# Moving VectorE's waiting instructions later in program order: evacuation, maximum, pick and transposed P between the block transposes of a decode-attention kernel

## The chip, the cores and the metric

The kernel runs on one core of one Trainium2 chip. Times are device microseconds (us) of that core, quoted as medians of the runs; a profiled execution gives the trace ("the span" is the time from its first to its last instruction, 1.2 to 2.5 us less than the run's time in these runs). The experiments ran in several rounds on different chips; the kernel before was timed again in each round, with medians of 438.63 to 439.46 us.

## The reference

Two independent problems A and B of the same shape are computed and their outputs concatenated. Each is one decode step of attention over a sliding window of the last 4096 positions of a cache, batch 2, 32 query heads, 16 key heads of width 128:

```python
q = (x @ wq).reshape(B, Sq, Hq, Dh).transpose(0, 2, 1, 3)       # B=2, Sq=1, Hq=32, Dh=128
k = repeat(k_cache[:, :, Sk - W:, :], rep, axis=1)              # W=4096, rep=2, bf16
v = repeat(v_cache[:, :, Sk - W:, :], rep, axis=1)
p = softmax(einsum("bhqd,bhkd->bhqk", q, k) * Dh ** -0.5)
o = einsum("bhqk,bhkd->bhqd", p, v).transpose(0, 2, 1, 3).reshape(B, Sq, Hq * Dh) @ wo
```

The work per byte is small. What matters is that 153.1 MB (the caches' windows, wq and wo) have to be read once from HBM, the memory that holds the inputs. The loads bring them into SBUF, and the matmuls put their results into PSUM; these are the core's two memories in which the kernel declares its buffers (`sbuf_tensor`, `psum_tensor`).

## The kernel before

The caches are cut into 16 slabs (4 key heads of one batch element, 4.19 MB of K and as much of V each). Two slabs, one per batch element, make a group G; there are 8 groups, and one load of wo (1.18 MB) for each. Step `t` handles K slab `t` and V slab `i = t - 3`. An even step is the first of a pair, an odd one the second.

In a step, VectorE transposes the two halves of the K slab in blocks (X0, X1), and TensorE multiplies each half into the scores (S0, S1, 16 matmuls of 512 columns each). Then follow, for a group: the maximum (VectorE), two tiny GpSimd steps and a transpose on TensorE (Tm), its reduction (nM), a broadcast back through TensorE and the bias for the exponential (VectorE), the exponential on ScalarE (about 5 us), the block transpose of P (pT, VectorE), the sums (a matmul and VectorE), PV on TensorE, its evacuation from PSUM (VectorE, two instructions), a matmul that gathers the diagonal blocks (dg), its pick (VectorE: A, then oP), and the output projection (TensorE).

VectorE needs half of `xt` free before it can transpose into it, so X(t, h) waits for S(t-1, h). The program order of each engine is the order of the calls in this loop:

```python
for t in range(NSLAB + LAG):                # NSLAB = 16, LAG = 3
    i = t - LAG; odd = t % 2 == 1; live = t < NSLAB
    Gb = t // 2 - 1 if not odd and t >= 2 and t <= NSLAB else None
    Gd = (t - 5) // 2 if odd and t >= 5 else None
    if live:
        make_X(t, 0); make_S(t, 0)
    if Gb is not None: make_bias(Gb)        # TensorE, then VectorE; the exponential behind it
    if Gd is not None: make_dg(Gd)          # TensorE, then VectorE (pick: A, oP)
    if live:
        make_X(t, 1); make_S(t, 1); ...
    if live and odd: make_max(t // 2)
    if Gb is not None: make_rsum(Gb); make_pT(Gb); make_sums(Gb)
    ...
    if i >= 0: make_PV(i); make_evac(i)
    if Gd is not None and Gd != NG - 2: make_proj(Gd) ...
    if live and odd: make_Tm(t // 2)        # with nM
```

The loads of K, V and wo are issued by SyncE, in one fixed order; a load whose buffer is still in use waits for a semaphore before it is issued (in the profile before SyncE stood 254.0 us in 16 waits for a transpose to free a slab's buffer, and 43.9 us in 5 waits in front of loads of wo). A ring of four buffers takes K and V slabs. wo has two buffers, so the load of wo G waits for projection G - 2:

```python
stream = []
for t in range(NSLAB + LAG):
    if t < NSLAB: stream.append(("K", t))
    if t >= LAG:
        i = t - LAG
        if i % 2 == 0 and i // 2 < NG - 2: stream.append(("W", i // 2))
        stream.append(("V", i))
...
def issue(key):
    if kind == "W":
        deps = [proj_op[i - 2]] if i >= 2 else []
    ...
    deps = [last_reader[prior[-1]]] if prior else first_deps[r]
```

## Time and profile before

| | before |
|---|---|
| time | 439.75 us (3 runs, 437.0 to 440.02), span of the profiled run 437.3 us |
| HBM read | 153.10 MB, 350 GB/s over the span |
| TensorE / VectorE busy | 57% / 49% of the span |
| a pair of steps, 153.0 to 204.3 us | 51.3 us |
| mean granted TensorE clock (1 is full speed) | 0.801 |

No engine is busy for much more than half the time. The chain that ended last, part 4 of the page, says that it passes through TensorE and VectorE in turn and hardly through DMA:

```profile
PE 52%; DVE 36%; DMA 8%; POOL 1%; ACT 1%; issue 1%; SPq 0%; DVEq 0%
```

The waits of VectorE in the kernel before (who waited for whom: total us, times, longest us) show where it stands:

```profile
DVE mx L456 <- PE st L242: 44.3, 8, 6.5
DVE tmp L551 <- PE tb L548: 43.6, 8, 7.1
DVE bias L474 <- PE tb L471: 39.7, 8, 6.0
DVE ssum L504 <- PE tb L501: 24.5, 7, 3.8
```

L456 is the maximum, L551 the first half of the pick (A), L474 the bias, L504 the sums. The timeline of VectorE in one pair (start us, duration us, line, what is written and read, idle time before it and its releaser) shows what these waits hold up:

```profile
152.98 4.42 DVE L422 STREAM_TRANSPOSE xt<-ring 128x4096 f32<-128x4096 f32 x1
162.93 0.23 DVE L474 SCALAR_TENSOR_TENSOR bias<-vmask,tb,offm 128x4 f32<-128x4 f32 x1 [5.53 <-PE tb L471]
163.08 4.44 DVE L422 STREAM_TRANSPOSE xt<-ring 128x4096 f32<-128x4096 f32 x1
...
177.76 4.43 DVE L422 STREAM_TRANSPOSE xt<-ring 128x4096 f32<-128x4096 f32 x1
189.14 0.42 DVE L551 TENSOR_TENSOR tmp<-tb,cm 128x256 f32<-128x256 f32 x1 [6.94 <-PE tb L548]
189.60 0.61 DVE L558 TENSOR_REDUCE oP<-tmp 128x16 bf16<-128x256 f32 x1
190.12 4.44 DVE L422 STREAM_TRANSPOSE xt<-ring 128x4096 f32<-128x4096 f32 x1
200.12 1.22 DVE L456 TENSOR_REDUCE mx<-st 128x2 f32<-128x1024 f32 x1 [5.56 <-PE st L242]
```

Read the first three lines: X0 ends at 157.4, and X1 could follow at once, its data lie in SBUF. But bias stands in front of it in program order, its input comes from a tiny transpose on TensorE (0.22 us, at 162.68) behind all of S0, and so X1 starts at 163.08. In the odd step the pick does the same. TensorE in turn stands still while X1 runs (its next group, at 167.57, had waited 4.68 us for it). The two engines take turns.

DMA follows from that: a buffer comes free late, so a load starts late. SyncE issues the loads (SPq is its queue), and the longest entry in its list of waits is the wait for a transpose to free a buffer:

```profile
SPq L369 <- DVE xt L422: 254.0, 16, 20.3
```

The windows view of a pair (window, its length, busy us and count of TensorE, its weight loads, VectorE, ScalarE and GpSimd, then granted clock, DMA share, GB/s):

```profile
205.00:256.00 51.00, 29.19 (x150) 7.04 (x110) 26.16 (x17) 4.98 (x8) 1.94 (x8) 0.80 0.84 352
```

From 5 to 135 us the same view gives 429 GB/s.

### The profile page before, as it was taken

Reading aid. Unit: us, or ns where it says so; the run is one execution under the profiler, and the core shown is the slowest. Engines: PE = TensorE matmul, PEld = TensorE weight load, DVE = VectorE, ACT = ScalarE, POOL = GpSimd, SP = SyncE. Lnnn points to the kernel's source line nnn. Section 1 sums busy time; section 2 is a strip of 40 time slices with the busy share of each in tenths; the row PEclk is TensorE's granted clock in tenths of the full one; section 3 lists DMA queues with packets and bytes.
Section 4 is the critical chain, followed back from the end, with each engine's and each line's share of the span. In section 5 each row is a group of like instructions: output and inputs, shape, how many; then the busy total and the mean of one; then the engine's idle time right before and its main releaser. Section 6 shows DMA issues by size and latency. Waiting matters only on the chain.

```text
span 437.3 us, 2617 instructions
## 1 busy us (share of the span) xinstructions
PE 247.6 (57%) x1299; PEld 60.3 (14%) x937; DVE 214.6 (49%) x138; ACT 44.4 (10%) x77; POOL 21.6 (5%) x82
## 2 busy tenths in 40 slices
PE   0553835494535845446466555368554474656487
PEld 0110101120111211011011111112111110111122
DVE  0207854645654345546443466534465455544343
ACT  1020004000400003000300004000040003100400
POOL 3000010000000000001000010000000010000100
PEclk9995988876876788769886688967888698866759
DMA  8999999999995898949989498967989497895900
GB/s 348 442 419 432 430 421 446 432 432 442 399 408 255 336 423 354 408 174 396 429 360 405 153 441 355 414 288 291 440 363 405 171 406 339 336 432 215 376 9 2
DMA packets 6660, 153.28 MB, mean 351 GB/s; under 512 B 748, under 2 KB 888, under 8 KB 1272
## 3 DMA queue, kind: packets, MB, share of 16 engines
q1 hardware_dynamic: 6628, 153.10, 83.3%
q8 instruction: 9, 0.15, 0.1%
q14 instruction: 3, 0.02, 0.0%
q10 hardware_dynamic: 20, 0.01, 0.0%
HBM read 153.10 MB, written 0.00 MB: 350 GB/s over the span
## 4 chain that ended last, share of the span: by engine, by line
PE 52%; DVE 36%; DMA 8%; POOL 1%; ACT 1%; issue 1%; SPq 0%; DVEq 0%
DVE xt L422 30%; PE st L448 20%; PE st L242 18%; DMA ring<-in_A_k_cache_dram 8%; PE ot L520 8%; DVE oR L542 2%; PE pj L583 2%; PE pj L242 2%; DVE tmp L541 1%; ACT pR L481 1%; PE tb L548 1%; DVE oP L558 1%; POOL zq L414 1%; PE tb L501 1%; DVE tmp L551 1%
## 5 line engine op out<-in xcount | busy, mean ns | idle before, releaser
L448 PE MATMUL st<-xt,zq 128*128 128x512 bf16 x256 | 132.3, 517 | 151.7 <-DVE xt L422 151.7
L422 DVE STREAM_TRANSPOSE xt<-ring 128x4096 f32<-128x4096 f32 x32 | 141.5, 4431 | 20.4 <-DMA ring<-in_A_k_cache_dram 18.5
L242 PE MATMUL st<-xt,zq 128*128 128x512 bf16 x256 | 129.1, 504 | 0.0
L481 ACT ACTIVATE pR<-st,bias 128x512 bf16<-128x512 f32 x32 | 39.7, 1402 | 305.6 <-DVE bias L474 305.6
L448 PEld LDWEIGHTS st<-xt,zq 128*128 128x128 bf16 x256 | 31.0, 121 | 280.1 <-DVE xt L422 160.7
L520 PE MATMUL ot<-ring,pT 128*32 128x512 bf16 x512 | 33.9, 412 | 0.0
L456 DVE TENSOR_REDUCE mx<-st 128x2 f32<-128x1024 f32 x8 | 9.8, 1225 | 44.3 <-PE st L242 44.3
L551 DVE TENSOR_TENSOR tmp<-tb,cm 128x256 f32<-128x256 f32 x8 | 3.4, 425 | 43.6 <-PE tb L548 43.6
L414 POOL TENSOR_TENSOR zq<-qs,bmask 128x64 bf16<-128x64 bf16 x32 | 8.7, 293 | 304.1 <-PE st L242 288.3
L490 DVE STREAM_TRANSPOSE pT<-pR 128x2048 bf16<-128x2048 bf16 x8 | 18.5, 2311 | 9.8 <-ACT pR L481 9.8
L541 DVE SCALAR_TENSOR_TENSOR tmp<-ot,rsb,dmask 128x512 f32<-128x512 f32 x16 | 12.0, 751 | 19.5 <-PE ot L520 19.5
L474 DVE SCALAR_TENSOR_TENSOR bias<-vmask,tb,offm 128x4 f32<-128x4 f32 x8 | 1.8, 227 | 39.7 <-PE tb L471 39.7
L542 DVE TENSOR_REDUCE oR<-tmp 128x128 f32<-128x512 f32 x16 | 16.4, 1026 | 0.6
L583 PE MATMUL pj<-wob,oP 128*2 128x288 bf16 x63 | 15.8, 286 | 0.5 <-DVE oP L558 0.5
L242 PE MATMUL pj<-wob,oP 128*2 128x288 bf16 x63 | 15.8, 286 | 0.0
L520 PEld LDWEIGHTS ot<-ring,pT 128*32 128x32 bf16 x512 | 12.8, 102 | 19.7 <-issue 10.4
L504 DVE TENSOR_REDUCE ssum<-tb 128x2 f32<-128x8 f32 x8 | 1.3, 162 | 24.5 <-PE tb L501 24.5
L275 PE MATMUL ot<-ring,pT 128*32 128x512 bf16 x36 | 8.3, 448 | 3.3 <-DMA ring<-in_B_wq_dram 2.8
L252 PE MATMUL tb<-ident_b,pR 8*128 8x8 bf16 x9 | 0.7, 199 | 15.3 <-DVE pR L213 15.3
L501 PE MATMUL tb<-rsum,m 128*128 128x8 f32 x16 | 3.2, 273 | 10.6 <-POOL rsum L495 10.6
L481 ACT ACTIVATION_READ_ACCUMULATOR pR<-st,bias 128x1 f32 x32 | 8.7, 271 | 0.0
L242 PE MATMUL pj<-ring,pT 128*32 128x512 bf16 x36 | 8.2, 444 | 0.0
(57 smaller groups left out, 62.1 us busy)
## 6 DMA issues: line engine op xcount, KB each, us to landing
ring<-in_A_k_cache_dram SPq DMA_DIRECT2D x8, 4096.0 KB, 24.1
ring<-in_A_v_cache_dram SPq DMA_DIRECT2D x8, 4096.0 KB, 16.6
ring<-in_B_k_cache_dram SPq DMA_DIRECT2D x8, 4096.0 KB, 12.8
ring<-in_B_v_cache_dram SPq DMA_DIRECT2D x7, 4096.0 KB, 14.8
ring<-in_A_wq_dram SPq DMA_DIRECT2D x1, 4608.0 KB, 13.6
ring<-in_B_wq_dram SPq DMA_DIRECT2D x1, 4608.0 KB, 24.0
wob<-in_A_wo_dram SPq DMA_DIRECT2D x4, 1152.0 KB, 12.3
wob<-in_B_wo_dram SPq DMA_DIRECT2D x3, 1152.0 KB, 6.3
```

The costliest lines, as they stand in the source:

```text
L242: return e.add_instruction(mybir.InstMatmult(name=nc.get_next_instruction_name(), engine=mybir.EngineType.PE, ins=[e.lower_ap(mv_), e.lowe ...
L275: last = e.matmul(o, wt, mv_, start=first, stop=True, skip_group_check=True)
L414: last = e.tensor_tensor(dst, src, msk, ALU.mult)
L422: Xop[(t, jh)] = dve(lambda e: e.transpose(xt[:, jh, :].bitcast(FP32).rearrange("p (kp x kt) -> p x kp kt", kp=2, kt=2), ring[:, r, jh * H ...
L448: last = e.matmul(ob, wt, mv_, start=first, stop=True, skip_group_check=True)
L456: ch[(G, "max")] = dve(lambda e: e.tensor_reduce(mx[:], st[:, :].rearrange("p (x t) -> p t x", t=2), AX.X, ALU.max), [Sop[(2 * G + 1, 1)]] ...
L481: last = e.activation(pR[:].rearrange("p (x k) -> p k x", k=4)[:, kv, :], st[:, :].rearrange("p (x t) -> p t x", t=2)[:, kv % 2, :], ACTF.Exp,
L490: pT_op[G] = dve(lambda e: e.transpose(pT[:, v, :].rearrange("p (w j q) -> p j w q", w=4, q=8), pR[:].rearrange("p (j w q) -> p j w q", w= ...
L520: last = e.matmul(OTB[32 * c:32 * c + 32, :], pT[:, v, base + 32 * c:base + 32 * c + 32], ring[:, r, jj * 128:(jj + 4) * 128], start=rd == ...
L541: evac_op[i] = dve(lambda e: e.scalar_tensor_tensor(tv, o, rsb[:, v, b:b + 1], dm, ALU.mult, ALU.mult), deps, "ev%d" % i)
L542: ch[(G, "red%d" % b)] = dve(lambda e: e.tensor_reduce(oR[:, b, :], tmp[:].rearrange("p (j d) -> p d j", j=4), AX.X, ALU.add), [evac_op[i] ...
L583: e.matmul(PJ[0], wt, wob[:, v, j, 0:NH], start=start and j == 0, stop=True, skip_group_check=True)
```

## The change

The intent is to put on VectorE, between X0 and X1, only work whose input is already there when X0 ends, and to move the instructions that wait for TensorE behind X1. For that, four things move down: the evacuation of PV(i) from the end of its step to the next step's gap, the maximum from the end of its odd step and the pick from the gap of its odd step to the gap of the next even step, and pT from its even step to the gap of the next odd step. The projection, which needs the pick, moves along; the dg matmul moves from the gap to the end of its odd step, Tm and nM follow the maximum, and the sums follow pT. Bias and sums stand behind X1. The diff, cut to its core (the maker functions are only split so that their TensorE and VectorE halves can be called apart):

```diff
             if live:
                 make_X(t, 0)
                 make_S(t, 0)
-            if Gb is not None:
-                make_bias(Gb)
-            if Gd is not None:
-                make_dg(Gd)
+            if 0 <= i - 1 and t <= NSLAB:
+                make_evac(i - 1)
+            if Gp is not None and not last:       # Gp = (t - 6) // 2, even steps
+                make_pick(Gp)
+            if Gc is not None:                    # Gc = (t - 2) // 2, even steps
+                make_max(Gc)
+            if Gs is not None:                    # Gs = (t - 3) // 2, odd steps
+                make_rsum(Gs)
+                make_pT(Gs)
+            if Gc is not None:
+                make_Tm_pe(Gc)
             if live:
                 make_X(t, 1)
                 make_S(t, 1)
 ...
-            if live and odd:
-                make_max(t // 2)
-            if Gb is not None:
-                make_rsum(Gb)
-                make_pT(Gb)
-                make_sums(Gb)
+            if Gc is not None:
+                make_nM(Gc)
+            if Gs is not None:
+                make_sums(Gs)
+            if Gd is not None:                    # Gd = (t - 5) // 2, odd steps
+                make_dg(Gd)
 ...
+            if Gp is not None and not last:
+                make_proj(Gp)
+ ...
+            if Gc is not None:
+                make_bias(Gc)
 ...
             if i >= 0:
                 make_PV(i)
-                make_evac(i)
-            if Gd is not None and Gd != NG - 2:
-                make_proj(Gd)
- ...
-            if live and odd:
-                make_Tm(t // 2)
+                if t >= NSLAB:
+                    make_evac(i)
```

More of the change, by code (lines that the diff above doesn't have):

```diff
@@ L397, in build_kernel @@
         ch = {}
+        tm_job = {}
+        dg_job = {}
         prev = lambda G, k: [ch[(G - 1, k)]] if (G - 1, k) in ch else []
@@ L459, in make_max, with make_Tm_pe, make_nM @@
             ch[(G, "pick")] = pool(lambda e: e.tensor_tensor(m1[:], mv[:, 0:1], mv[:, 1:2], ALU.add), [ch[(G, "mult")]] + prev(G, "Tm"), "pick%d" % G)
-        def make_Tm(G):
+        def make_Tm_pe(G):
             n, b, op = tb_job(lambda e, bank: e.transpose(bank[0:1, 0:128], m1[:, 0:1], ident_f[:]), "Tm%d" % G, [ch[(G, "pick")], p_ident_f])
             ch[(G, "Tm")] = op
+            tm_job[G] = (n, b)
+        def make_nM(G):
+            n, b = tm_job[G]
+            op = ch[(G, "Tm")]
             nm = dve(lambda e: e.tensor_reduce(nM[0:1, 0:16], b[0:1, 0:128].rearrange("o (a w) -> o w a", a=8), AX.X, ALU.max, negate=True),
@@ L550, in make_dg, with make_pick @@
             ch[(G, "dg")] = op
+            dg_job[G] = (n, bank)
+        def make_pick(G):
+            v = G % 2
+            n, bank = dg_job[G]
+            op = ch[(G, "dg")]
             a = dve(lambda e: e.tensor_tensor(
@@ L605, in build_kernel @@
             live = t < NSLAB
-            Gb = t // 2 - 1 if not odd and t >= 2 and t <= NSLAB else None
+            Gc = (t - 2) // 2 if not odd and t >= 2 else None
+            Gs = (t - 3) // 2 if odd and t >= 3 else None
             Gd = (t - 5) // 2 if odd and t >= 5 else None
+            Gp = (t - 6) // 2 if not odd and t >= 6 else None
+            if Gc is not None and Gc >= NG:
+                Gc = None
+            if Gs is not None and Gs >= NG:
+                Gs = None
+            last = t == NSLAB + LAG - 1
             if live:
@@ L619, in build_kernel @@
                     make_Z(t + 2)
-            if live and odd:
-                make_max(t // 2)
-            if Gb is not None:
-                make_rsum(Gb)
-                make_pT(Gb)
-                make_sums(Gb)
-            if t == NSLAB + LAG - 1:
+            if Gc is not None:
[4 more added lines that the diff above has]
+                make_dg(Gd)
+                if Gd == NG - 2:
+                    make_pick(Gd)
+            if Gp is not None and not last:
+                make_proj(Gp)
+                if (Gp + 1) % GP == 0:
+                    make_E(Gp // GP)
+            if Gc is not None:
+                make_bias(Gc)
+            if last:
                 filler(4)
@@ L629, in build_kernel @@
                 make_PV(i)
-                make_evac(i)
-            if Gd is not None and Gd != NG - 2:
-                make_proj(Gd)
-                if (Gd + 1) % GP == 0:
-                    make_E(Gd // GP)
-            if live and odd:
-                make_Tm(t // 2)
+                if t >= NSLAB:
+                    make_evac(i)
         filler(3)
@@ L639, in build_kernel @@
         make_dg(NG - 1)
+        make_pick(NG - 1)
         filler(3)
```

## The prediction

> What bounds the kernel now. The steps run in series. In the chain of waits the transposes take 30% of the span, the score matmuls 38%, and DMA only 8%. In the timeline from 153.0 to 204.3 us one pair of steps takes 51.3 us. VectorE is busy for only about 26.2 us of such a pair, TensorE for 29.2 (windows view). The list of VectorE's waits says why: in each pair it stands at bias for 5.5 us, at the pick's first half (A) for 6.9, at maximum for 5.6, at the sum for 3.6, at the evacuation for about 2.1. Each waits for a TensorE result queued behind score matmuls, and the next 4.43 us transpose stands behind it. [...]the trace agrees (after 5.5 us idle bias starts at 162.93 and the transpose behind it at 163.08).
>
> DMA: 429 GB/s from 5 to 135 us, then 352 in each pair, with holes
>
> What changes. No work is added or removed. Bias (even steps) and A (odd steps) leave the place between the two transposes; evacuation, pick, maximum and pT go there, by which time their inputs are done. Expected compute time from the first transpose's start:
> - odd step: 4.45 + evacuation 1.8 + pT 2.35 + 4.45 = 13.1, second score group about 5.1, sums and reciprocal 0.6: 18.8.
> - even step: 4.45 + 1.8 + pick 1.05 + maximum 1.25 + 4.45 = 13.1, score group 5.1, projection 2.1, bias 0.5: 20.8.
> A pair: 39.6 us instead of 51.3. The bias and the sums still stand in front of the next first transpose, so half of the serialization remains.
>
> A pair moves 17.96 MB (4 slabs of 4.19 MB and one wo of 1.18): 41.8 us at 429 GB/s. So DMA becomes the bound.
>
> A new wait: the projection also moves, from an odd step to the end of the next even step. The in-order DMA queue holds wo behind projection G-2, and behind wo stand the next V and K. So once in a pair the queue runs nearly dry: K of the even step lands, 20.2 us of step to the projection, 1.2 us from issue to the first bytes, then wo, V, K, 22.2 us: about 44 us a pair.
>
> Sum. Until K6 lands DMA is saturated: 53.7 MB, about 126 us. Four pairs of 44 (K14 at 302), then K15 and the last four V without wo in between; exp, pT, PV in series after K15, and V15 can only be issued after PV13: last PV at about 369, and from there 8.5 us to the end as before. Span 378, time 379 us.
>
> PREDICTED time 379 us, range 367 to 392. Faster by over 2% 0.97, within 2% 0.02, slower 0.01.
>
> What would show it: VectorE waits for bias and sums only at the step's end, 5 to 7 us each; transposes appear as waiting for DMA in even steps; the DMA queue's largest waits are wo for the projection in each pair; pairs of 42 to 45 us.
>
> What would make it wrong: the TensorE clock (0.5 after idle, the score group 3.8 to 6.9 us by it; [...]here 0.43 us per matmul, then 0.24); warm second groups give 42 us pairs and about 370. Cold ones give 46 and 390. A longer tail.

Two passages that did not come from a trace or run of this case are cut and marked. No term of the sum goes with them: it still comes to a span of 378 us and a time of 379. What the trace of the kernel before shows of the hardware that the prediction speaks of:

- The clock: the granted clock was 0.50 from 157.4 to 160.4 us, at 0.43 us from matmul to matmul, and 1.00 from 160.7 to 162.6, at 0.24. Each of the 22 score groups from 130.60 to 397.30 us began at 0.40 to 0.43 us from matmul to matmul, after TensorE had stood idle for 4.68 to 6.27 us. The range of 3.8 to 6.9 us for a group is an estimate: sixteen times 0.24 and sixteen times 0.43.
- From issue to the first bytes: a load of K was issued at 194.59 us, and DMA moved 0 GB/s until 195.80: 1.2 us.
- The order of the loads: wo was issued at 152.56 us, V at 152.94 and K at 167.54, in the order of the list.

## The result

| | before | after |
|---|---|---|
| time, median | 439.19 us (4 runs, 437.0 to 440.02) | 381.36 us (4 runs, 380.03 to 383.39) |
| HBM read over the span | 350 GB/s | 401 GB/s |
| a pair of steps | 51.3 us | 44.2 us (129.29 to 306.18 us are four pairs) |
| mean granted TensorE clock | 0.801 | 0.848 |

The ratio is 0.869, with a 95% interval of 0.864 to 0.875. The result is correct.

The profiled spans differ by 55.9 us. Counted by the start of the even X0 of steps 6 and 14 (152.98 and 357.94 us before, 129.29 and 306.18 after), 23.7 us of this lie before step 6, 28.1 in the four pairs from there, and 4.1 after step 14 begins.

The chain that ended last now goes mostly through DMA:

```profile
DMA 50%; DVE 22%; PE 18%; issue 7%; ACT 1%; SPq 1%; POOL 0%; DVEq 0%
```

The waits of VectorE after the change. The pick and the maximum are gone from the top; the transposes (L424) now wait for DMA:

```profile
DVE bias L481 <- PE tb L478: 43.1, 7, 7.6
DVE ssum L511 <- PE tb L508: 37.4, 7, 6.8
DVE xt L424 <- DMA ring<-in_A_k_cache_dram: 27.0, 4, 18.1
DVE xt L424 <- DMA ring<-in_B_k_cache_dram: 21.5, 6, 5.6
```

The timeline of VectorE in a pair after the change:

```profile
129.29 4.45 DVE L424 STREAM_TRANSPOSE xt<-ring 128x4096 f32<-128x4096 f32 x1 [5.00 <-DMA ring<-in_A_k_cache_dram]
...
136.46 1.22 DVE L458 TENSOR_REDUCE mx<-st 128x2 f32<-128x1024 f32 x1
137.59 4.44 DVE L424 STREAM_TRANSPOSE xt<-ring 128x4096 f32<-128x4096 f32 x1
...
149.69 0.23 DVE L481 SCALAR_TENSOR_TENSOR bias<-vmask,tb,offm 128x4 f32<-128x4 f32 x1 [7.51 <-PE tb L478]
149.84 4.44 DVE L424 STREAM_TRANSPOSE xt<-ring 128x4096 f32<-128x4096 f32 x1
...
155.91 2.30 DVE L497 STREAM_TRANSPOSE pT<-pR 128x2048 bf16<-128x2048 bf16 x1
158.13 4.40 DVE L424 STREAM_TRANSPOSE xt<-ring 128x4096 f32<-128x4096 f32 x1
168.10 0.17 DVE L511 TENSOR_REDUCE ssum<-tb 128x2 f32<-128x8 f32 x1 [5.57 <-PE tb L508]
...
174.04 4.45 DVE L424 STREAM_TRANSPOSE xt<-ring 128x4096 f32<-128x4096 f32 x1 [5.57 <-DMA ring<-in_B_k_cache_dram]
```

Between X0 and X1 VectorE never waits. One wait per step is left, at its end (bias in even steps, sums in odd ones), and the even step's X0 then waits for its K slab. The compute part of the pair is 20.55 us (129.29 to 149.84) and 18.6 us (149.84 to 168.4), 39.2 us; the rest of the 44.75 us of this pair is waiting for DMA.

That DMA is not full shows in windows of one us in the same pair (the last two columns are DMA's share and GB/s):

```profile
146.00:147.00 1.00, 1.00 (x6) 0.19 (x2) 0.00 (x0) 0.00 (x0) 0.00 (x0) 1.00 0.27 98
147.00:148.00 1.00, 1.00 (x8) 0.25 (x4) 0.00 (x0) 0.00 (x0) 0.47 (x2) 1.00 0.08 33
148.00:149.00 1.00, 1.00 (x11) 0.36 (x5) 0.00 (x0) 0.00 (x0) 0.60 (x2) 1.00 0.00 0
149.00:150.00 1.00, 1.00 (x14) 0.42 (x14) 0.31 (x2) 0.05 (x1) 0.00 (x0) 1.00 0.00 0
```

And this is what ends the hole, in SyncE's timeline. The load of wo comes first, at 149.53, when the projection on TensorE is done; a V slab and a K slab are issued right behind it, though their buffers had long been free (the V load's since PV ended at 126.7 us, the K load's since X1 ended at 142.0):

```profile
149.53 0.33 SPq L353 DMA_DIRECT2D wob<-in_A_wo_dram  x1
149.91 0.54 SPq L369 DMA_DIRECT2D ring<-in_A_v_cache_dram  x1
150.49 0.61 SPq L369 DMA_DIRECT2D ring<-in_B_k_cache_dram  x1
```

In SyncE's own list of waits this one (L353 issues wo; it is put down to the last TensorE instruction before it, the bias's transpose) is the longest:

```profile
SPq L353 <- PE tb L478: 134.3, 5, 30.2
```

### The profile page after: what moved, and what is told of

Same layout as the page of the kernel before. It is cut to its first block, busy times and chain, and to the rows that moved or that the text cites. A ratio compares the mean times of both kernels' runs of the same rounds, so it can differ in the third digit from the quotient of the medians.

```text
span 381.4 us, 2626 instructions
## 1 busy us (share of the span) xinstructions
PE 236.0 (62%) x1299; PEld 58.6 (15%) x937; DVE 212.2 (56%) x138; ACT 44.7 (12%) x77; POOL 22.0 (6%) x82
## 4 chain that ended last, share of the span: by engine, by line
DMA 50%; DVE 22%; PE 18%; issue 7%; ACT 1%; SPq 1%; POOL 0%; DVEq 0%
DMA ring<-in_A_k_cache_dram 25%; DMA ring<-in_B_k_cache_dram 25%; DVE xt L424 13%; PE st L450 5%; PE st L242 5%; PE pj L596 2%; PE pj L242 2%; DVE oR L549 2%; DVE mx L458 2%; PE ot L527 2%; DVE tmp L548 2%; ACT pR L488 1%; DVE pT L497 1%; DVE oP L571 1%; DVE tmp L564 1%
## 5 line engine op out<-in xcount | busy, mean ns | idle before, releaser
L450 PE MATMUL st<-xt,zq 128*128 128x512 bf16 x256 | 124.1, 485 | 109.1 <-DVE xt L424 109.1
L424 DVE STREAM_TRANSPOSE xt<-ring 128x4096 f32<-128x4096 f32 x32 | 141.6, 4431 | 49.8 <-DMA ring<-in_A_k_cache_dram 27.0
L242 PE MATMUL st<-xt,zq 128*128 128x512 bf16 x256 | 122.6, 479 | 0.0
L450 PEld LDWEIGHTS st<-xt,zq 128*128 128x128 bf16 x256 | 29.4, 115 | 234.1 <-DVE xt L424 125.9
L527 PE MATMUL ot<-ring,pT 128*32 128x512 bf16 x512 | 32.3, 396 | 0.0
L596 PE MATMUL pj<-wob,oP 128*2 128x288 bf16 x63 | 17.3, 305 | 0.5 <-DVE oP L571 0.5
L242 PE MATMUL pj<-wob,oP 128*2 128x288 bf16 x63 | 17.3, 306 | 0.0
L275 PE MATMUL ot<-ring,pT 128*32 128x512 bf16 x36 | 8.9, 477 | 2.2 <-DMA ring<-in_B_wq_dram 1.7
L213 DVE TENSOR_TENSOR pR<-tmp,hmask 8x1152 bf16<-8x1152 bf16 x1 | 1.3, 1347 | 12.7 <-DMA tmp<-in_B_x_dram 12.7
L555 PE MATMUL tb<-oR,selx 128*128 128x256 f32 x16 | 6.1, 466 | 3.3 <-DVE ssum L511 3.3
```

What stands on the lines that cost most here:

```text
L242: return e.add_instruction(mybir.InstMatmult(name=nc.get_next_instruction_name(), engine=mybir.EngineType.PE, ins=[e.lower_ap(mv_), e.lowe ...
L275: last = e.matmul(o, wt, mv_, start=first, stop=True, skip_group_check=True)
L424: Xop[(t, jh)] = dve(lambda e: e.transpose(xt[:, jh, :].bitcast(FP32).rearrange("p (kp x kt) -> p x kp kt", kp=2, kt=2), ring[:, r, jh * H ...
L450: last = e.matmul(ob, wt, mv_, start=first, stop=True, skip_group_check=True)
L527: last = e.matmul(OTB[32 * c:32 * c + 32, :], pT[:, v, base + 32 * c:base + 32 * c + 32], ring[:, r, jj * 128:(jj + 4) * 128], start=rd == ...
L596: e.matmul(PJ[0], wt, wob[:, v, j, 0:NH], start=start and j == 0, stop=True, skip_group_check=True)
```

## The experiments

The theory has three parts: the time came from VectorE's order (T1); the changed kernel is held by DMA and by the wo load in its queue (T2); the granted clock only sets the length of the links of the chain (T3). Rivals are named at each run. Each heading says on which kernel the edit was made.

### e1: the wo load one step later (on after)

```diff
-                if i % 2 == 0 and i // 2 < NG - 2:
+                if i % 2 == 1 and i // 2 < NG - 2:
                     stream.append(("W", i // 2))
```

> The kernel after the change, with each wo load put one step later in the DMA queue (behind K of the next even step, before the second V of its pair), nothing else. Theory (the queue is held each pair by the wo load that waits for the projection of two groups before): the five SP waits of about 30 us for the projection vanish, the hole in DMA once a pair (121 GB/s at 145 to 150 us) vanishes, a pair of steps takes 41.8 us instead of 44.2, and the time falls by five times 2.4 us to about 369 us. Rival (the hole comes from the ring of four slots or from the compute chain, wo only stands in it): SP waits the same time at the next V or K, time 379 to 383 us.

Measured: 369.97 us, ratio to before 0.844 (0.841 to 0.848). The pairs took 41.66, 41.64, 41.68 and 41.65 us (126.53 to 293.16 us), and the windows view of one of them shows DMA full:

```profile
210.00:252.00 42.00, 29.24 (x166) 7.19 (x118) 26.31 (x17) 5.01 (x8) 2.19 (x8) 0.80 1.01 433
```

SyncE's waits for the projection fell from 134.3 to 40.1 us in total, and DMA no longer runs dry:

```profile
SPq L353 <- PE tb L478: 40.1, 5, 13.3
```

So the hole came from the place of wo in SyncE's order of loads, not from the four ring buffers: the same ring now keeps DMA full. The profiled span is 13.4 us shorter (381.4 to 368.0): 2.8 us of it before the even X0 of step 6, where the second wo load no longer stands in front of K6, and 10.3 us in the four pairs. This supports T2, with the number expected (41.8 us, 369 us).

### e2: the same wo move in the kernel before

The diff is that of e1, made on the kernel before.

> The kernel before with the same one-step-later wo load. Theory: the kernel before is bound by its compute chain of 51.3 us a pair, so keeping DMA fuller is worth nothing: 436 to 441 us. Rival (DMA order was a limit in the kernel before too): 10 us or more faster.

Measured: 439.78 us, ratio 1.002 (0.999 to 1.005). The kernel before was not held by the order of its loads; the same edit that saves 11 us after the change saves nothing before it.

### e3: the pick alone (on before)

```diff
-            if Gd is not None:
-                make_dg(Gd)
             if live:
                 make_X(t, 1)
                 make_S(t, 1)
                 ...
+            if Gd is not None:
+                make_dg(Gd)
```

> The kernel before with only the dg matmul and the pick (A, oP) moved from between the two transposes of an odd step to behind the second score group. Theory (VectorE's order is what serializes): the wait of 6.9 us at A between the transposes goes, the second transpose follows the first, the two score groups of odd steps run back to back, a pair takes 44 to 45 us instead of 51.3, time about 385 to 395 us. Rival (all moves are needed together; the wait just moves to the next instruction, the maximum): within 2% of 439 us.

Measured: 394.85 us, ratio 0.900 (0.897 to 0.903), pairs of 44.4 us (215.69 to 260.07). In VectorE's timeline the two transposes of the odd step now follow each other (one merged line of 8.76 us):

```profile
215.69 8.76 DVE L422 STREAM_TRANSPOSE xt<-ring 128x4096 f32<-128x4096 f32 x2
229.59 0.42 DVE L551 TENSOR_TENSOR tmp<-tb,cm 128x256 f32<-128x256 f32 x1 [5.14 <-PE tb L548]
```

The wait did not move on in full: A waits 5.14 us behind both transposes, and the maximum behind it no longer waits. Moving the pick (two instructions a pair, with their dg matmul) gives 44 of the 58 us. One other cure was not run: dg ahead of S0 on TensorE, with the pick where it was. The rival, that only all the moves together pay, falls. In the pairs the pick alone even gives what the whole change gives, 44.4 us against 44.2, where the changed kernel is held by its wo load. The changed kernel's profiled span is 12.8 us shorter, and this comes from the time before step 6, whose even X0 starts at 129.29 us instead of 145.12, less 3.6 us lost after step 14 begins.

### e4: the bias alone (on before)

```diff
-            if Gb is not None:
-                make_bias(Gb)
 ...
             if live:
                 make_X(t, 1)
                 make_S(t, 1)
                 ...
+            if Gb is not None:
+                make_bias(Gb)
             if live and odd:
                 make_max(t // 2)
```

> The kernel before with only the bias moved from between the two transposes of an even step to behind the second score group; pT stays in the same step. Theory: the wait at bias goes, but pT then stands on VectorE waiting for the whole exponential (about 5 us) with the next transposes behind it, so the even step gets about 2 us longer (24.8 to 26.7): 445 to 460 us. Rival (every move of a waiting instruction out of the gap between transposes pays by itself): about 5 us per pair less, 395 to 405 us.

Measured: 439.84 us, ratio 1.003 (0.999 to 1.007): no gain, which excludes the rival, but not the loss that I had put a number on either. VectorE's timeline:

```profile
202.38 8.75 DVE L422 STREAM_TRANSPOSE xt<-ring 128x4096 f32<-128x4096 f32 x2
215.97 0.23 DVE L474 SCALAR_TENSOR_TENSOR bias<-vmask,tb,offm 128x4 f32<-128x4 f32 x1 [4.84 <-PE tb L471]
221.20 2.31 DVE L490 STREAM_TRANSPOSE pT<-pR 128x2048 bf16<-128x2048 bf16 x1 [5.01 <-ACT pR L481]
```

pT, still in the same step, stands waiting for the whole exponential, 5.01 us, and eats what the bias gave. The even step took 25.0 us (202.38 to 227.41) instead of 24.8; I had expected 26.7. So moving the bias alone does not pay, and the change moves pT with it; that the two moved without the other instructions would pay was not run.

### e5: the end of the kernel reordered (on e1)

```diff
+            end = t == NSLAB
+            if end: make_max(Gc)                  # before evacuation and pick
-            if 0 <= i - 1 and t <= NSLAB:
+            if 0 <= i - 1 and t < NSLAB:
                 make_evac(i - 1)
 ...
                 make_nM(Gc)
+            if end:
+                make_bias(Gc)                     # before the projection of group 5
+                make_evac(i - 1)
```

> e1_wo_later with the last group's chain pulled ahead in the step after the last K slab: its maximum before the evacuation and the pick, its bias before the projection of group 5 and before that evacuation. In e1 the last bias is computed at 343.8 us although its score group ended at about 332; DMA ends at 358.6 and the span at 368.0. Theory: the last exponential starts about 7 us earlier, the tail then hangs on the last V and wo bytes, which land as before, so the span ends about 5 to 6 us after DMA: time 365 to 367 us. Rival (the tail is set by the last DMA alone): 369 to 371 us as e1.

Measured: 367.12 us, ratio 0.837 (0.834 to 0.840), against e1's 0.844. The last bias came at 336.76 instead of 343.83 us, as expected, but only 3 us of the 7 reached the end, and the time lies just above the expected 365 to 367. The projection of group 6 waits for its wo bytes until 357.5 us and then runs at a granted clock of 0.53 (359 to 361 us; 0.24 us from matmul to matmul, 0.12 in the last projection) in front of the last dg, so the last pick stands at 362.4.

### e6: three quarters of each V slab (on e1)

```diff
+                cl = 96 if kind == "V" and len(cuts) == 1 else c1
-                def f(e, c0=c0, c1=c1, sm=sm):
+                def f(e, c0=c0, c1=cl, sm=sm):
```

> e1_wo_later with three quarters of each V slab loaded (the last quarter of the buffer keeps older data; the result is wrong on purpose; the last V slab is whole). Bytes per pair fall from 17.96 to 15.86 MB, 37.0 us at 429 GB/s. Theory (e1 is bound by DMA at 41.8 us a pair, and the compute chain behind it needs about 39.2): pairs of 39 to 40 us, DMA no longer full, time about 353 to 360 us. Rival (DMA is still the bound at any such size, compute far below): pairs of 37.0 us, time about 336 to 345 us. Second rival (e1 is not bound by DMA at all): 368 to 371 us.

Measured: 354.65 us; the result is wrong. With 12% fewer bytes in a pair, the pairs took 37.8 and 38.0 us (starts of the even X0 at 202.44, 240.21 and 278.19) in the second half and 39 to 40 in the first; no even X0 in steady state waited for DMA any more; each starts right behind the sums, and these wait for TensorE:

```profile
239.93 0.17 DVE L513 TENSOR_REDUCE ssum<-tb 128x2 f32<-128x8 f32 x1 [5.68 <-PE tb L510]
...
240.21 4.43 DVE L426 STREAM_TRANSPOSE xt<-ring 128x4096 f32<-128x4096 f32 x1
```

The compute chain behind e1's DMA bound is thus 38 to 40 us, as T2 says. DMA in the window from 202 to 240 us still ran at 430 GB/s, so the two limits lie close together here, and this run tells compute-bound from DMA-bound less sharply than I had hoped: 37.0 was the number of the rival for the pair. Its time, 336 to 345 us, is excluded.

### e7: ten idle matmuls ahead of each score group (on before)

```diff
+        def keep_warm(t):
+            def f(e):
+                w = qs[:].rearrange("d p w -> d (p w)")
+                last = e.matmul(OTB[:, :], ones_b[:, :], w, start=True, stop=True, ...)
+                for _ in range(9):
+                    last = mm_held(e, OTB[:, :], ones_b[:, :], w, True)
+                return last
+            pe(f, [qs_ev, q_ev[0]] + ([evac_op[t - LAG - 1]] if t > LAG else []), "warm")
 ...
                 make_X(t, 0)
+                keep_warm(t)
                 make_S(t, 0)
 ...
                 make_X(t, 1)
+                keep_warm(t)
                 make_S(t, 1)
```

> The kernel before with ten matmuls of no use into the free PV bank ahead of each score group, in time in which TensorE waits for the transpose; order of VectorE untouched. It asks what the granted clock alone is worth. Theory (the order of VectorE serializes, the clock only sets the length of the links): score groups take 3.8 to 4.5 us instead of 5.2 to 6.5, all four of a pair lie on the chain, so 4 to 6 us a pair: 395 to 415 us, with the same waits in the same places and idle VectorE. Rival (the change gained by the clock, 0.80 to 0.85): with a clock near 1 this kernel is as fast as the changed one or faster, 381 us or less.

Measured: 428.87 us, ratio 0.979 (0.973 to 0.986), verdict unclear at 2%, and outside what I expected. The ten ran in 2.3 us (212.36 to 214.68 us, some 0.21 us from one to the next), and then TensorE stood for 2.4 us or more before its group. Of the four groups from 207 to 242 us three, for instance the one at 207.02, still began at 0.43 us from matmul to matmul, after 2.42 to 3.36 us of standing; the one at 231.78 began at 0.24, after 3.09. The edit did not do what it was for. It does say one thing: a mean granted clock of 0.889, above the changed kernel's 0.848, came with 428.87 us.

### e8: the evacuation put back (on after)

```diff
-            if 0 <= i - 1 and t <= NSLAB:
-                make_evac(i - 1)
 ...
             if i >= 0:
                 make_PV(i)
-                if t >= NSLAB:
-                    make_evac(i)
+                make_evac(i)
```

> The kernel after the change with the evacuation put back to the end of its own step; all other moves kept. Theory: the odd step's chain grows to about 21.4 us and the even one's to 22.7 (44.1 a pair), while the wo load that holds the queue comes about 1.6 us earlier in the even step; as the pair already takes 44.2 us because of that load, almost nothing changes: 378 to 386 us. Rival (the evacuation's place is a main part of the gain): 395 us or more.

Measured: 375.13 us, ratio to before 0.855 (0.853 to 0.857), against 0.869 of the changed kernel. Undoing this part of the change made it faster by 6 us; nothing in my expectation allowed for that. Four pairs took 172.5 us (129.90 to 302.38) instead of 176.9, and the time from X0 of step 14 to the end 71.3 instead of 75.2 us. So the gain is in both places, about half each. From the even X0 to the issue of wo it is now 17 us instead of 18.8 to 20.3, for instance:

```profile
215.60 4.45 DVE L424 STREAM_TRANSPOSE xt<-ring 128x4096 f32<-128x4096 f32 x1 [3.04 <-DMA ring<-in_B_k_cache_dram]
...
232.66 0.33 SPq L353 DMA_DIRECT2D wob<-in_B_wo_dram  x1
```

It is shorter because 1.8 us of evacuation no longer lie in front of X1 and with it of S1 and the projection.

### e9: e1 with the evacuation put back

The diff is that of e8, made on e1.

> e1_wo_later with the evacuation put back to the end of its own step. Without the hold of wo the DMA bound is 41.8 us a pair and the compute chain with this order about 44.1, so now the evacuation's place should show: pairs of about 44 us, 380 to 385 us against e1's 370. Rival (the evacuation's place never matters): 368 to 372 us.

Measured: 367.37 us, ratio 0.837 (0.834 to 0.840), against e1's 0.844. Expected were 380 to 385. The compute chain I had summed was too long: an odd step took 19.6 us (191.13 to 210.77) and not 21.4, because S1 was shorter: the sums wait 4.15 us behind X1 (202.09 to 206.24 us), in e1 up to 5.7, and sixteen matmuls at 0.24 us take 3.8 us, at 0.43 us 6.9. DMA stays full as in e1 (430 and 432 GB/s in the windows from 168 to 252 us; pairs of 40.3 to 41.6 us), the even X0 of step 14 comes at 293.44 instead of 293.16, and all of the gain lies behind it: 72.0 us from there to the end instead of 74.8.

### e10: the parts that paid, together

e9, and the order at the end changed: the last maximum, the pick of group 5, Tm and nM right behind the last score group and ahead of the evacuation, the last bias ahead of the projection of group 5, and the last dg and pick ahead of the projection of group 6.

```diff
                 make_PV(i)
-                make_evac(i)
+                if t == NSLAB - 1:
+                    make_max(NG - 1); make_pick((t - 5) // 2)
+                    make_Tm_pe(NG - 1); make_nM(NG - 1)
+                else:
+                    make_evac(i)
 ...
+            if t == NSLAB:
+                make_bias(Gc); make_evac(i - 1)   # ahead of make_proj
 ...
         filler(3)
-        make_proj(NG - 2)
         make_dg(NG - 1)
         make_pick(NG - 1)
-        filler(3)
+        make_proj(NG - 2)
         make_proj(NG - 1)
```

> wo one step later and the evacuation at its own step's end (as e9, 367.4 us), and the end of the kernel reordered: the last group's maximum, the pick of group 5 and the last bias right behind the last score group, before the evacuation and before the projection of group 5; the last dg and pick before the projection of group 6. In e9 the last bias stands at 342.5 us and the last V is in use at 355.1, DMA ends at about 358.6, the span at 365.4. Theory: bias at about 337.5, the last PV then waits for its V bytes only, last wo lands at about 359, two projections and the store behind it: span about 363 us, time 363 to 365.5. Rival (nothing left but DMA and a fixed tail): 367 to 368 as e9.

Measured: 366.31 us (5 runs, 364.76 to 366.9), ratio 0.835 (0.832 to 0.838), the fastest correct kernel by its median, 1.1 us ahead of e9, of which it is not clear of noise, and above the expected 363 to 365.5. The last PV did wait for its V bytes only (its last four matmuls at 354.62 us) and the pick came at 358.66, but TensorE's granted clock was 0.50 from 355 to 361 us, and the two projections took until 363.8. The gain of the earlier bias was given back there.

### e11: sixteen idle matmuls instead of ten (on before)

The diff is that of e7 with `range(15)`.

> e7 with sixteen instead of ten idle matmuls ahead of each score group. In e7 the ten ran in 2.3 us right behind the group before and TensorE then stood still for 2.5 to 3.4 us again, so three of four groups still began at the half clock. Sixteen at full clock fill about 3.8 us of the 4.4. Theory (serial chain, clock sets the length of the links): groups of 3.8 us, 5 to 6 us a pair less than the 51.3, time 395 to 410 us, VectorE's waits in the same places, about 4 us each. Rival (the gain of the change is the clock): 381 us or less. If cold matmuls outlast the transpose: 430 or more, and nothing is told.

Measured: 404.65 us, ratio 0.922 (0.919 to 0.926). Now the granted clock held at 1.00 (windows view of a pair):

```profile
198.00:242.00 44.00, 35.81 (x211) 6.37 (x112) 26.10 (x15) 5.02 (x8) 2.16 (x8) 1.00 0.94 400
```

The pair took 44.6 us (197.92 to 242.53) with VectorE's order untouched, and VectorE still waited at bias 4.18, at A 4.46 and at the maximum 4.04 us. T3 holds: with a serial chain the clock (a mean of 0.97 over the profile, against 0.801) is worth 34 us, but at 0.97 the old order still takes 23 us more than the new order at 0.848. All of these 23 us lie before step 6, whose even X0 comes at 153.31 us here and at 129.29 in the changed kernel. In the later pairs the two are level, 44.6 and 44.2 us, as the changed kernel is held there by its wo load; e1, without that hold and at a mean clock of 0.861, takes 41.65.

### e12: eight idle matmuls between the two groups (on after)

```diff
                 make_X(t, 1)
+                keep_warm(t)                      # eight matmuls, into the free PV bank
                 make_S(t, 1)
```

> The kernel after the change, evacuation where the change put it, with eight idle matmuls (into the free PV bank) ahead of the second score group only. It asks why e8 gained 6 us, where no change was expected: in e8 the second groups took 3.8 us, in the changed kernel 5.2, and TensorE's pause ahead of them is about 1.8 us longer there. Theory (the pause lets the clock fall, and so the projection and with it the wo load come later): second groups of 3.8 to 4 us, wo issued about 1.4 us earlier in the even step, 374 to 378 us. Rival (e8 gained by VectorE's order or by the end of the kernel alone): 380 to 383 us.

Measured: 381.56 us, ratio 0.871 (0.867 to 0.875), the same as the changed kernel. The second groups did become short (the one from 186.78 us at 0.24 us from matmul to matmul throughout), and the wo load was issued at 18.8 us after the even X0 in every pair instead of 18.8 and 20.3 in turn. But the pairs stayed at 44.5 us, and the time saved on VectorE became wait for K (line of its timeline):

```profile
173.98 4.45 DVE L424 STREAM_TRANSPOSE xt<-ring 128x4096 f32<-128x4096 f32 x1 [8.09 <-DMA ring<-in_B_k_cache_dram]
```

From the issue of wo to the even X0 it took 25.5 to 26.0 us here and 24.4 to 25.0 in the changed kernel. So the clock of the second group does not explain e8's gain in the pairs, and that theory falls. Nor does the pause alone decide how a group begins: in the changed kernel the second groups at 142.09 and 230.62 us began at 0.40 to 0.43 us from matmul to matmul after pauses of 2.16 and 2.06 us, those at 186.84 and 275.39 at 0.24 after 2.33 and 2.24. What remains for e8's pairs is the place of the evacuation itself (wo at 17 us instead of 18.8); why 0.75 us earlier on average bought nothing in e12, with DMA's lost time about the same (one minus DMA's share, summed over windows of one us: 2.2 us a pair in both), is left open.

## Why the prediction was right

The measured 381.36 us lies 2.4 us from the predicted 379, and the change is faster by over 2%, which had a chance of 0.97. The sum can be checked term by term:

| term | predicted | measured |
|---|---|---|
| even X0 of step 6 (K6 there) | about 126 us | 129.3 us |
| four pairs | 4 x 44 us | 176.9 us (44.75, 43.79, 44.77, 43.58) |
| last PV done | about 369 us | 372.9 us |
| from there to the end | 8.5 us | 8.5 us |
| span | 378 us | 381.4 us |

- **What bounded the kernel before: right.** The serial turn-taking of VectorE and TensorE. e3 takes the pick, with its dg matmul, out of the gap and gains 44 us; e2 shows that feeding DMA better gains nothing.
- **The compute chain after the change: right.** 18.8 and 20.8 us were predicted for the two steps, 18.6 and 20.55 were measured (149.84 to 168.5 and 129.29 to 149.84 us). In the next pair it was 19.8 and 19.1, in sum the same: 39.2 and 38.9 us against 39.6.
- **DMA as the new bound: right.** e1 runs at 41.65 us a pair, predicted from 17.96 MB at 429 GB/s as 41.8. Over stretches in which DMA is full the traces, with loads of 4.19 MB from SyncE, show 429 GB/s before (5 to 135 us) and 433 in e1 (210 to 252 us).
- **The wait that the moved projection creates: right, and it was the part that is not seen in the diff.** The projection moved from an odd step to the end of the next even one, and with it the wo load that stands in front of V and K. e1 removes just this and gains 11.4 us by the medians, about 2.6 us in each pair. The 44 us were a sum of two terms, and here there was some luck, as their errors cancel: from the even X0 to the issue of wo 20.2 us were predicted and 19.6 measured on average (18.8 to 20.3), from there to the next even X0 23.4 (1.2 and 22.2) were predicted and 24.7 measured (24.4 to 25.0).
- **The start: 3 us too short.** K6 was put at 126 us; it was used at 129.3. The second wo load, which e1 takes from ahead of K6 (126.5 us there), is not the reason, as the predicted 53.7 MB contain it. Some 2 us are, by estimate, the start of the transfers: in the first slice of the page, 9.5 us long, DMA moved 337 GB/s instead of 430. The rest is open. This offset carries through the table to the end.
- **Implied, and not so: that every move helps.** The prediction put the evacuation's 1.8 us on the path of both steps and did not ask whether it would cost less where it was. e8 and e9 show that it costs: 6 us in the changed kernel, 2.6 us once wo is out of the way. It lengthens the path X0, X1, S1, on which the projection and the last group's chain hang, and e8's shorter way to the wo load (17 us) shows that part; that at the end of its own step it fills time for which nobody waits is my reading.
- **The clock: the branch that was named did not come true.** The prediction named warm second groups as worth about 9 us (pairs of 42 us). e12 warmed them and gained nothing: the pairs stayed at 44.5 us, with longer waits for K; why is open. In the kernel before, a mean clock of 0.97 instead of 0.801 is worth 34 us (e11).

## What to carry to other kernels

VectorE ran its instructions in program order here: bias, 0.23 us long, waited 5.53 us for TensorE, and X1, whose data lay ready, started behind it at 163.08 us. Where an engine does so, put into the gap between two long instructions only what has its input already; moving a tiny instruction that waits can need its consumers to move too (e4). After moving work to a later place, look for what waits for it in another queue: here a weight load behind the moved projection held up the two slab loads behind it (issued at 149.53, 149.91 and 150.49 us), and putting it two places later in the load order gained 11 us more. When the chain is serial, test the granted clock separately from the order, and undo the parts of a change one at a time even when the whole is a success: here one part cost 6 us.
